# First loads, constants and late rows of an FFT and MoE kernel issued by GpSimd, zero rows stored later

## The chip, the cores and the metric

One core of a Trainium2 chip runs the kernel. The metric is the device time of one execution in microseconds: the median of the runs. A profiled execution gives, beside its time, the span from its first to its last instruction, the busy time of every engine, each DMA transfer and the clock granted to TensorE.

## The reference

An FFT along the sequence, a filter in the frequency domain, the inverse FFT, and then a mixture of experts in which each token goes to one expert, by the order of the sorted logits and a capacity of N / E tokens for each expert.

```python
X = np.fft.rfft(x, axis=1)                  # x: 8 x 2496 x 256, fp32
Y = X * (filt_r + 1j * filt_i)[None, :, :]
y = np.fft.irfft(Y, n=x.shape[1], axis=1)
x = y.reshape(B * S, D)                     # 19968 tokens x 256
logits = x @ w_gate                         # 8 experts
for idx in np.argsort(-logits.flatten()):   # greedy, cap = N // E
    tok, e = idx // E, idx % E
    ...
for e in range(E):
    h = np.maximum(x[mask[e]] @ w1[e], 0)   # 256 -> 1024
    out[mask[e]] = h @ w2[e]                # 1024 -> 256
```

## The kernel before

The sequence of 2496 is 39 x 64. The forward FFT is a step of 39 points (`s1`, a matmul with the constant `cS1`) and a step of 64 points (`s2`, with the per-column constants `cW`), then the product with the filter `F` (VectorE makes `P` and `Q`, GpSimd combines them at L246 and L247). `tr` transposes the result, adds the gate's columns (`pv`), and splits it into a high and a low part (`yh`, `yl`, at L278 and L279); `inv1` is the inverse step of 64 points with the constants `cE`, also in a high and a low part (`cEh`, `cEl`). Its result goes through the buffer `zt` (four of them) to DRAM (`zd`), and comes back as rows `z` for the inverse step of 39 points (`inv2_parts`, L399), whose result `xo` is stored as tokens `xs`. Each of the eight batch rows is a block `b`: its x comes in two halves `xr` (L208, each load cut into 112 partitions and 5), `s1` takes it in 11 tiles, `s2` in 5 groups of two halves, `tr` and `inv1` in 10 steps.

`run` (L406) gives each piece a slot and a priority and writes them out in that order; then the framework's scheduler sets the order on each engine by its own model of time. A queue's instructions start in order. Loads and stores from SP and ScalarE go round eight completion lanes (`DMAHW0` to `7` in the orders below), those from GpSimd round eight others (`DMASW0` to `7`); a transfer waits until the one before it on its lane has landed.

Before, SP issues all of x, the filter, the zero rows of `zd` (`zeros`, L195), the stores of `zt` and the loads of `z`. GpSimd issues the constants `cEh` and `cEl` in three parts (`load_E`, L189), and ahead of each stands a copy of one element of a product `P` into the target, so that the load waits for that product: the gate of that load.

Late in the FFT the last six blocks' rows `z` are kept back (`rest`, 30 of them): `more_z` (L354) and `more_z2` load eight of them into the places of `F`, `cW`, `Vh` and `Vl` when these are no longer read, and the other loads follow as `z` buffers come free. They are worked off beside the routing phase of the first expert. Then come the experts' matmuls (L854, L897) up to the end.

Of the kernel before, what the change touches and what calls it, by code (L numbers as in the profile page):

```python
# [12 lines left out]
B, N, D, E8, FF = 8, 2496, 256, 8, 1024  # L13

N1, N2, K1, J = 39, 64, 20, 64
# [114 lines left out]
class Fft:  # L130


    def __init__(s, tc, i, xs, zd, lg, pp):
        s.tc, s.nc, s.i, s.xs, s.zd, s.lg, s.pp = tc, tc.nc, i, xs, zd, lg, pp
        s.zw = s.zo = s.y7 = s.y9 = None
        s.xos = []
        s.nload = s.nstore = 0
        s.st_x = tc.nc.sync
        s.cps = tc.nc.vector.tensor_copy, tc.nc.scalar.copy
        s.y1c = {}  # L140
        s.Y1, s.yt, s.yd, s.z, s.xr, s.vs = {}, {}, {}, {}, {}, {}
# [29 lines left out]
    def consts2(s):  # L171
        nc, i = s.nc, s.i
        t = lambda n, sh, dt=F32: s.cp.tile(sh, dt, name=n)
        s.Vh, s.Vl = (s.cp.tile([128, K1, 64], F32R, name=n, tag=n, bufs=1) for n in ("Vh", "Vl"))
        s.id, s.gate = t("fid", [128, 128]), t("gate", [128, 2, 32])
        s.zero = s.zp.tile([120, 5, D], F32, name="xo", tag="xo", bufs=2)[:40, 0]
        s.cE = [t(n, [128, K1, 128], F32R) for n in ("cEh", "cEl")]
        for k, g in zip("FxFxFxFxFx", (0, 0, 1, 1, 2, 2, 3, 3, 4, 4)):
            if k == "F":
                nc.sync.dma_start(s.F[:, g], i['filt'][g].rearrange("p (h k j) -> p h k j", h=2, k=4))  # L180
            else:
                s.load_x(1, g // 3, *((g, 3) if g < 3 else (g - 3, 2)))
        make_identity(nc, s.id)
        nc.gpsimd.memset(s.gate, 0.0)
        nc.gpsimd.memset(s.zero, 0.0)
        for h in range(2):
            nc.scalar.dma_start(s.gate[:, h, :8], i['moe_w_gate'][128*h:128*h+128])

    def load_E(s, g, k0, k1):  # L189

        for c, nme in zip(s.cE, ("cEh", "cEl")):
            s.nc.gpsimd.tensor_copy(c[:1, k0, :1], s.yt[0, g, 0][:1, 0, :1])
            s.nc.gpsimd.dma_start(c[:, k0:k1], s.i[nme].rearrange("p (k q) -> p k q", k=K1)[:, k0:k1])

    def zeros(s):  # L195
        for zd in s.zd:
            s.nc.sync.dma_start(zd[:, N2:], s.zero.unsqueeze(1).to_broadcast([40, 2, D]))

    def load_x(s, b, h, k=0, parts=1):

        w = 24 - 5*h
        if k == 0:
            s.xr[b, h] = s.xp.tile([117, w, 2, N2], F32, name=f"xr{h}", bufs=2)
        xr = s.xr[b, h]
        v = s.i['x'][b].rearrange("p (q c n) -> p q c n", c=2, n=N2)
        q0, q1 = 4*((w+3)//4*k//parts), min(4*((w+3)//4*(k+1)//parts), w)
        for r in (slice(0, 112), slice(112, 117)):
            s.nc.sync.dma_start(xr[r, q0:q1], v[r, 24*h+q0:24*h+q1])  # L208

    def s1(s, b, t):  # L210

# [140 lines left out]
            nc.vector.tensor_copy(s.lg[:, b0:b1, g0:g1], p[:117].rearrange("p g (b e) -> p b g e", e=8))  # L352

    def more_z(s, units):  # L354

        f = s.wp.tile([128, 4, 5, D], F32, name="F", tag="F", bufs=1)
        w = s.wp.tile([128, 2, 5, D], F32, name="cW", tag="cW", bufs=1)
        y = s.wp.tile([128, 4, 5, D], F32, name="Y1", tag="Y1", bufs=2)
        s.xos = [y[:120, k] for k in range(4)]
        zs = [f[:120, k] for k in range(4)] + [w[:120, k] for k in range(2)]  # L360
        for u, z in zip(units, zs):
            s.load_z(*u, z)
# [5 lines left out]
    def load_z(s, b, t, z=None):  # L368
        g0, g1 = 5*t, min(5*t+5, G)
        if z is None:  # L370
            z = s.new_z((b, t) in s.rest)
        s.z[b, t] = z
        s.nc.sync.dma_start(z[:, :g1-g0], s.zd[b].rearrange("a (i g) c -> (a i) g c", i=3)[:, g0:g1])

    def new_z(s, late):
        zp, n = (s.zp, 3) if not late or s.nload % (3 + NZ) < 3 else (s.zw, NZ)
# [29 lines left out]
    def run(s, cp, wp, xp, ps, freed, prep, rest):  # L406
        s.cp, s.wp, s.xp, s.ps, s.rest = cp, wp, xp, ps, rest
        ev = []
        at = lambda slot, pr, fn, *a: ev.append((slot, pr, len(ev), fn, a))
        at(-12, 0, s.consts)  # L410
        for k in range(5):
            at(-12, 0, s.load_x, 0, k // 3, *((k, 3) if k < 3 else (k - 3, 2)))
        at(-12, 2, s.consts2)
        for g in range(1, 5):
            at(2*g - 2.1, 2.5, s.second, g)
        at(2.5, 1.5, s.load_E, 1, 0, 4)
        at(4.5, 1.5, s.load_E, 2, 4, 12)
        at(6.5, 1.5, s.load_E, 3, 12, K1)
        at(12, 9, s.zeros)
        for b in range(B):  # L420
            o = 10*b
            for t in range(11):
                at(o - 10 + t*10/11, 2, s.s1, b, t)
            if b + 2 < B:
                for h in range(2):
                    at(o - 4.4 + 4.5*h, 8, s.load_x, b + 2, h)
            for g in range(5):
                for dh in range(2):
                    at(o + 2*g + dh, 1, s.s2, b, g, dh)
                at(o + 2*g + 4.5, 3.5, s.trv, b, g)  # L430
            for q in range(10):
                at(o + q + 3, 3, s.tr, b, q)
                if b < B - 1 or q < 2:
                    at(o + q + I1, 4, s.inv1, b, q)
            for t in range(5):
                if b < B - NPOST:
                    z = Z0 + ZS * (5*b + t)
                    at(z - 4, 6, s.load_z, b, t)
                    at(z, 5, s.inv2, b, t)
        at(10*B - 9.5, 0, freed)  # L440
        for g in range(5):
            at(10*B - V1 + g*V1D, 3.8, s.v1, g, 0, B - 1)
            at(10*B - 5.2 + 2*g, 3.6, s.v1, g, B - 1, B)
        at(10*B - V2, 3.8, s.v2, 0, B - 1)
        at(10*B - V3, 3.8, s.v3, 0, B - 1)
        at(10*B - VP, 3.8, prep, 0, G * (B - 1))
        def act():
            s.cps = (s.nc.scalar.copy,) * 2
        at(10*B - AC, 0, act)
        for u in rest[:3]:  # L450
            at(10*B - 15, 9, s.load_z, *u)
        at(10*B - 0.8, 9, s.more_z, rest[3+NZ:9+NZ])
        at(10*B + 2.9, 3.61, s.more_z2, rest[9+NZ:3+NZ+MZ])
        at(10*B + 2.9, 3.6, s.v2, B - 1, B)
        at(10*B + 2.9, 3.62, s.v3, B - 1, B)
        at(10*B + 2.9, 3.64, prep, S - G, S)
        for q in (2, 3, 4):
            at(10*B + 2.9, 3.7 + 0.01 * q, s.inv1, B - 1, q)
        for e in sorted(ev, key=lambda e: e[:3]):
            e[3](*e[4])  # L460
# [665 lines left out]
```

## Time and profile before

| | |
|---|---|
| median of 3 runs | 1446.38 us (1446.09 to 1447.12) |
| profiled execution | 1445.38 us |
| its span | 1443.6 us |
| TensorE busy | 1386.9 us, 96% of the span |
| VectorE, ScalarE, GpSimd busy | 900.5, 680.5, 486.1 us |
| mean granted clock | 0.981 |

The FFT of the eight blocks takes the first 340 us, the late rows and the routing of the first expert go to about 434 us, and the rest are the experts. TensorE is busy nearly throughout, so time can only be won or lost where it waits, or where its clock is at the lower level. DMA busy share over 1 in a window means that transfers of the 16 engines overlap.

### The profile page before, as it was taken

To read this page: it belongs to the slowest core of one execution; us is meant where nothing else is said; L and a number is where in the kernel's file an instruction comes from. 1 tells how busy PE (TensorE), PEld (TensorE's weight loads), DVE (VectorE), ACT (ScalarE), POOL (GpSimd) and SP (SyncE) were. 2 spreads that over 40 slices of the span, in tenths; PEclk is the share of its full clock that TensorE was granted. 3 is DMA by queue.
4 is the path that set the end of the run, shared out by engine and by line. 5 is a ranking of instruction groups with operands and counts; after the bars stand their busy time and mean duration, and the time that the engine had idled before them with its cause. 6 is when DMAs were issued, how large, how long until landed. Compare 5 with 4: busy or idle time off the path is not lost. (4 is left out here: it accounts for less than half of the span.)

```text
span 1443.6 us, 27297 instructions
## 1 busy us (share of the span) xinstructions
PE 1386.9 (96%) x10338; PEld 1215.5 (84%) x10338; DVE 900.5 (62%) x2568; ACT 680.5 (47%) x1658; POOL 486.1 (34%) x538
## 2 busy tenths in 40 slices
PE   8799999998887999999999999999999999999998
PEld 7799988986446889888898988889898899899988
DVE  6476777776556778767856877776867735323231
ACT  6567666744464236325524533533633635433232
POOL 2343333442004315413531641433414333323212
PEclk9899999998997999999999999999999999999999
DMA  9977775558893103102112112111201321111100
GB/s 246 242 204 196 206 193 145 144 128 196 319 327 108 47 19 114 57 21 96 61 40 77 56 54 79 52 51 40 100 29 54 127 74 46 43 44 54 36 23 28
DMA packets 57992, 150.66 MB, mean 104 GB/s; under 512 B 10999, under 2 KB 32247, under 8 KB 54409
## 3 DMA queue, kind: packets, MB, share of 16 engines
q1 hardware_dynamic: 29068, 66.86, 17.5%
q0 software_dynamic: 18416, 60.37, 12.7%
q10 hardware_dynamic: 10377, 21.68, 4.6%
q8 instruction: 82, 1.34, 0.4%
q14 instruction: 49, 0.40, 0.1%
HBM read 85.23 MB, written 63.70 MB: 103 GB/s over the span
## 5 line engine op out<-in xcount | busy, mean ns | idle before, releaser
L897 PE MATMUL py<-w1h,hl 128*128 128x256 f32 x2496 | 485.8, 287 | 1.0 <-DVE hl L865 0.7
L897 PEld LDWEIGHTS py<-w1h,hl 128*128 128x128 f32 x2496 | 403.0, 191 | 7.3 <-issue 3.2
L897 PE MATMUL py<-w1l,hl 128*128 128x256 f32 (+1 forms) x1280 | 359.5, 283 | 0.0
L908 POOL DMA_INDIRECT out<-y,oid x160 | 168.8, 1055 | 507.0 <-ACT y L907 458.7
L860 ACT ACTIVATE hl<-pz 128x512 fp32r<-128x512 f32 (+1 forms) x320 | 187.4, 587 | 226.9 <-PE pz L854 203.6
L854 PE MATMUL pz<-xo,w0h 128*128 128x512 f32 (+1 forms) x640 | 263.9, 412 | 3.3 <-DVE hl L862 1.8
L862 DVE SCALAR_TENSOR_TENSOR hl<-pz,hl 128x512 fp32r<-128x512 f32 x256 | 175.4, 689 | 144.5 <-ACT hl L860 143.2
L854 PE MATMUL pz<-z,w0h 128*128 128x512 f32 (+1 forms) x640 | 248.7, 389 | 0.2 <-DVE z L836 0.2
L854 PE MATMUL pz<-xo,w0l 128*128 128x512 f32 (+1 forms) x640 | 248.5, 388 | 0.0
L897 PEld LDWEIGHTS py<-w1l,hl 128*128 128x128 f32 (+1 forms) x1280 | 241.7, 189 | 1.9
L818 POOL DMA_INDIRECT xg<-xs,xid x160 | 168.7, 1055 | 131.5 <-issue 51.5
L907 ACT COPY y<-py 128x256 f32<-128x256 f32 x152 | 56.6, 372 | 305.9 <-PE py L897 265.4
L854 PEld LDWEIGHTS pz<-xo,w0l 128*128 128x128 f32 x640 | 120.8, 189 | 24.0
L854 PEld LDWEIGHTS pz<-xo,w0h 128*128 128x128 f32 x640 | 121.7, 190 | 21.6 <-DVE hl L862 2.2
L854 PEld LDWEIGHTS pz<-z,w0h 128*128 128x128 f32 x640 | 121.6, 190 | 16.0 <-DVE z L836 0.9
L226 ACT COPY Y<-p 64x240 f32<-64x240 f32 (+1 forms) x302 | 115.3, 382 | 25.2 <-PE p L220 17.8
L246 POOL TENSOR_TENSOR P<-P 128x256 f32<-128x256 f32 x80 | 58.8, 735 | 184.9 <-DVE P L244 184.8
L557 DVE TENSOR_TENSOR Gm<-M,thr 117x1232 bf16<-117x1232 f32 (+2 forms) x80 | 105.5, 1329 | 0.2
L220 PE MATMUL p<-cS,xr 117*128 117x120 f32 x688 | 96.4, 279 | 9.2 <-DMA xr<-x 7.6
L220 PEld LDWEIGHTS p<-cS,xr 117*128 117x128 f32 x688 | 87.3, 195 | 13.7 <-issue 8.4
L238 PE MATMUL p<-cW,Y 128*128 128x128 f32 x640 | 89.9, 277 | 0.5 <-DVE Q L245 0.5
L238 PEld LDWEIGHTS p<-cW,Y 128*128 128x128 f32 x640 | 80.9, 192 | 6.0 <-issue 4.1
(220 smaller groups left out, 2013.7 us busy)
## 6 DMA issues: line engine op xcount, KB each, us to landing
z<-zd SPq DMA_DIRECT2D x26, 600.0 KB
zd<-zt SPq DMA_DIRECT2D x120, 128.0 KB
xs<-xo ACTq DMA_DIRECT2D x18, 600.0 KB
xr<-x SPq DMA_DIRECT2D x6, 1344.0 KB
xr<-x SPq DMA_DIRECT2D x6, 1064.0 KB
zd<-zt ACTq DMA_DIRECT2D x40, 128.0 KB
xs<-xo SPq DMA_DIRECT2D x8, 600.0 KB
xs<-Y ACTq DMA_DIRECT2D x6, 600.0 KB
```

The source lines that it names most:

```text
L220: s.lastmm = nc.tensor.matmul(p[:, q-q0, :120], xv[:, q-24*h], s.cS1, start=True, stop=True).ins
L226: c = (nc.vector.tensor_copy if (t == 5 if b else cp) else nc.scalar.copy)(dst, src)
L238: nc.tensor.matmul(p[:, k], s.Y1[b][:, 4*g+k, dh*128:dh*128+128], s.cW[:, 4*g+k], start=True, stop=True)
L246: nc.gpsimd.tensor_tensor(P[:, :, :64], P[:, :, :64], P[:, :, 64:], op=OP.subtract)
L557: nc.vector.tensor_tensor(Gm[:, s0:s1, :m], s.M[:, s0:s1].unsqueeze(2).to_broadcast([117, s1 - s0, m]), thr[:117].unsqueeze(1).to_broadcas ...
L818: s.lastg = s.nc.gpsimd.indirect_dma_start(out=xg[:n], out_offset=None, in_=s.xs, in_offset=bass.IndirectOffsetOnAxis(ap=ids[0][:n, t:t+1] ...
L854: nc.tensor.matmul(p[:, :n], w[:, sl], x[:, k, :n], start=m == 0, stop=m == 5)
L860: s.lasta = nc.scalar.activation(h[:, :n], p[:, :n], AF.Relu).ins
L862: s.R.low = nc.vector.scalar_tensor_tensor(l[:, :n], p[:, :n], 0.0, h[:, :n].bitcast(F32), op0=OP.max, op1=OP.subtract).ins
L897: nc.tensor.matmul(p[:a.stop-a.start], hs[g][f][:, a], b[:, 256*f:256*f+256], start=m == 0, stop=m == 8 * len(terms) - 1, skip_group_check ...
L907: s.lasta = nc.scalar.copy(y, p).ins
L908: st = nc.gpsimd.indirect_dma_start(out=out_rows, out_offset=bass.IndirectOffsetOnAxis(ap=ids[1][:w, 4*g+t:4*g+t+1], axis=0), in_=y[:w], i ...
```

## The change

The loads of the 112-partition parts of x of blocks 0 and 1, the filter and the inverse constants are issued by GpSimd. The constants' gates are gone, and their three parts stand between the filter groups and x of block 1. The identity is made after the second load in `consts2`'s list for block 1 instead of after all. The zero rows are held until `s.y1a`, the last copy of `s1` that ScalarE has when they are written. From `more_z` on, GpSimd issues the loads of `z` too.

```diff
-        s.st_x = tc.nc.sync
+        s.st_x, s.late = tc.nc.sync, False
...
-        for k, g in zip("FxFxFxFxFx", (0, 0, 1, 1, 2, 2, 3, 3, 4, 4)):
+        for k, g in zip("FxFxxFExFExFE", (0, 0, 1, 1, 2, 2, 0, 3, 3, 1, 4, 4, 2)):
             if k == "F":
-                nc.sync.dma_start(s.F[:, g], i['filt'][g].rearrange("p (h k j) -> p h k j", h=2, k=4))
+                nc.gpsimd.dma_start(s.F[:, g], i['filt'][g].rearrange("p (h k j) -> p h k j", h=2, k=4))
+            elif k == "E":
+                s.load_E(*((0, 4), (4, 12), (12, K1))[g])
             else:
                 s.load_x(1, g // 3, *((g, 3) if g < 3 else (g - 3, 2)))
-        make_identity(nc, s.id)
+            if (k, g) == ("x", 1):
+                make_identity(nc, s.id)
...
-    def load_E(s, g, k0, k1):
+    def load_E(s, k0, k1):
         for c, nme in zip(s.cE, ("cEh", "cEl")):
-            s.nc.gpsimd.tensor_copy(c[:1, k0, :1], s.yt[0, g, 0][:1, 0, :1])
             s.nc.gpsimd.dma_start(c[:, k0:k1], s.i[nme].rearrange("p (k q) -> p k q", k=K1)[:, k0:k1])
     def zeros(s):
-        for zd in s.zd:
-            s.nc.sync.dma_start(zd[:, N2:], s.zero.unsqueeze(1).to_broadcast([40, 2, D]))
+        with s.tc.issue_after(s.y1a):
+            for zd in s.zd:
+                s.nc.sync.dma_start(zd[:, N2:], s.zero.unsqueeze(1).to_broadcast([40, 2, D]))
...
-            s.nc.sync.dma_start(xr[r, q0:q1], v[r, 24*h+q0:24*h+q1])
+            (s.nc.gpsimd if b < 2 and r.start == 0 else s.nc.sync).dma_start(xr[r, q0:q1], v[r, 24*h+q0:24*h+q1])
...
     def more_z(s, units):
+        s.late = True
...
-        s.nc.sync.dma_start(z[:, :g1-g0], s.zd[b].rearrange("a (i g) c -> (a i) g c", i=3)[:, g0:g1])
+        (s.nc.gpsimd if s.late else s.nc.sync).dma_start(z[:, :g1-g0], s.zd[b].rearrange("a (i g) c -> (a i) g c", i=3)[:, g0:g1])
...
-        at(2.5, 1.5, s.load_E, 1, 0, 4)
-        at(4.5, 1.5, s.load_E, 2, 4, 12)
-        at(6.5, 1.5, s.load_E, 3, 12, K1)
```

The scheduler then orders the instructions anew. GpSimd at the start, before: the gates (L192) and loads (L193) of the first constants stand between the products of the first filter groups.

```order
L246 TENSOR_TENSOR P<-P 128x4x64 [waits DVE_49]
L192 CAST cEh<-P 1x1 [waits Pool_49]
L192 CAST cEl<-P 1x1
L247 TENSOR_TENSOR P<-Q 128x4x64 [waits DVE_49]
L193 DMA cEh<-cEh 128x512 [waits Pool_49]
L193 DMA cEl<-cEl 128x512 [waits Pool_49]
```

The same place after, the end of the loads: `xr_152` is the second half of block 1, `cEh` and `cEl` of 128x512 are the first part of the constants.

```order
L195 DMA cEh<-cEh 128x512 [waits DMASW3_49]
L195 DMA cEl<-cEl 128x512 [waits DMASW4_49]
L211 DMA xr_152<-x 112x1024 [waits DMASW5_49]
L180 DMA F<-filt 128x1024 [waits DMASW6_49]
L195 DMA cEh<-cEh 128x1024 [waits DMASW7_49]
L195 DMA cEl<-cEl 128x1024 [waits DMASW0_49]
L211 DMA xr_152<-x 112x1408 [waits DMASW1_49]
L180 DMA F<-filt 128x1024 [waits DMASW2_49]
L195 DMA cEh<-cEh 128x1024 [waits DMASW3_49]
L195 DMA cEl<-cEl 128x1024 [waits DMASW4_49]
L187 MEMSET gate 128x64
```

The first products (L249) come behind these rows, after the memsets and the identity; 21 loads stand ahead of them, of which the first eight (block 0's five, filter group 0, block 1's first piece, filter group 1) wait for no lane.

SP at the start, before: block 1's last piece (`xr_147`), then block 2's halves (`xr_225`, `xr_292`), then the zero rows.

```order
L180 DMA F<-filt 128x1024 [waits DMAHW3_49]
L208 DMA xr_147<-x 112x1408 [waits DMAHW4_49]
L208 DMA xr_147<-x 5x1408 [waits DMAHW5_49]
L208 DMA xr_225<-x 112x3072 [waits DMAHW6_49,PE_49]
L208 DMA xr_225<-x 5x3072 [waits DMAHW7_49]
L208 DMA xr_292<-x 112x2432 [waits DMAHW0_49,PE_49]
L208 DMA xr_292<-x 5x2432 [waits DMAHW1_49]
L197 DMA zd_60<-xo 40x2x256 [waits DMAHW2_49,Pool_49]
```

After, block 2 is `xr_231` and `xr_298`, block 3's first half `xr_479`.

```order
L211 DMA xr_152<-x 5x1408 [waits DMAHW4_49]
L211 DMA xr_231<-x 112x3072 [waits DMASW2_49,DMASW1_49,DMAHW5_49,DMASW0_49,PE_49]
L211 DMA xr_231<-x 5x3072 [waits DMAHW6_49]
L211 DMA xr_298<-x 112x2432 [waits DMASW4_49,DMAHW7_49,DMASW3_49,PE_49]
L211 DMA xr_298<-x 5x2432 [waits DMAHW0_49]
L200 DMA zd_60<-xo 40x2x256 [waits DMAHW2_49,Pool_49]
L200 DMA zd_61<-xo 40x2x256 [waits DMAHW4_49]
L211 DMA xr_479<-x 112x3072 [waits DMASW6_49,DMAHW1_49,DMASW1_49,DMAHW5_49,DMASW0_49,PE_49]
```

Block 2's x no longer stands behind block 1's x and the filter, and two of the eight zero rows stand ahead of block 3.

TensorE at the same time, before: the first tile of block 2 (`p_697`) is followed by inverse steps (L293) and gate columns (L266).

```order
L220 MATMUL p_697<-cS_87,xr_225 128x120 [waits DMAHW6_49,DMAHW7_49,PE_49,Activation_49]
L220 MATMUL p_697<-cS_87,xr_225 128x120 x3
L293 MATMUL pa<-yh,cEh 128x256 [waits DMASW0_49]
L293 MATMUL pa<-yl,cEh 128x256
L257 MATMUL pa<-fid,P 128x128 x4
L266 MATMUL pv<-P,gate 32x128 x8
```

After: tiles 8 to 10 of block 1 (`p_576`, `p_627`, `p_671`) and 0 and 1 of block 2 (`p_691`, `p_738`) stand in a row, and the first gate columns (L269) behind them; inverse steps (L296) come later still.

```order
L223 MATMUL p_576<-cS_87,xr_152 128x120 [waits DMAHW4_49,DMASW1_49,Activation_49]
L223 MATMUL p_576<-cS_87,xr_152 128x120 x3
L223 MATMUL p_627<-cS_87,xr_152 128x120 [waits Activation_49]
L223 MATMUL p_627<-cS_87,xr_152 128x120 x3
L223 MATMUL p_671<-cS_87,xr_152 128x120 [waits PE_49,Activation_49]
L223 MATMUL p_671<-cS_87,xr_152 128x120 x2
L223 MATMUL p_691<-cS_87,xr_231 128x120 [waits DMAHW5_49,DMAHW6_49,PE_49,Activation_49]
L223 MATMUL p_691<-cS_87,xr_231 128x120 x3
L223 MATMUL p_738<-cS_87,xr_231 128x120 [waits PE_49,Activation_49]
L223 MATMUL p_738<-cS_87,xr_231 128x120 x3
L269 MATMUL pv<-P,gate 32x128 [waits DMAHW1_49]
```

Up to that point ten second steps have been issued before (one of them in progress) and seven after, four transposes before and two after, two gate groups and two inverse steps before and none after.

GpSimd's late rows, before: the last two products of block 7, then the splits of its last inverse steps (L279) and nothing between them.

```order
L246 TENSOR_TENSOR P<-P 128x4x64 [waits DVE_49]
L247 TENSOR_TENSOR P<-Q 128x4x64 [waits DVE_49,Pool_49]
L279 TENSOR_TENSOR yl<-Y_3932,yh 128x512 [waits PE_49,Activation_49] x4
L279 TENSOR_TENSOR yl<-P,yh 128x512 [waits PE_49,Activation_49]
L998 COPY sidx<-xo 1x1 [waits Activation_49,Pool_49]
```

After: four loads into `F`'s place stand between these two products, and the loads of `z` among the splits.

```order
L249 TENSOR_TENSOR P<-P 128x4x64 [waits DVE_49]
L376 DMA F<-zd_63 120x1280 [waits DMASW2_49,DMASW0_49,DVE_49]
L376 DMA F<-zd_63 120x1280
L376 DMA F<-zd_63 120x512
L376 DMA F<-zd_64 120x1280 [waits DMASW3_49]
L250 TENSOR_TENSOR P<-Q 128x4x64 [waits Pool_49]
L376 DMA Vh<-zd_64 120x1280 [waits DMASW4_49,DVE_49,PE_49]
L376 DMA Vl<-zd_64 120x512 [waits DMASW5_49,PE_49]
L282 TENSOR_TENSOR yl<-Y_3926,yh 128x512 [waits PE_49,Activation_49] x3
```

## Rows read from the trace of the kernel before

**Rows 1.** The page, part 1, first entry: busy us (share of the span) xinstructions.

```profile
PE 1386.9 (96%) x10338; PEld 1215.5 (84%) x10338; DVE 900.5 (62%) x2568; ACT 680.5 (47%) x1658; POOL 486.1 (34%) x538
```

**Rows 2.** TensorE's waits, 0 to 100 us: us in total, times, longest us.

```profile
PE p L220 <- DMA xr<-x: 7.6, 5, 3.7
PE pa L293 <- DVE zt L305: 3.9, 1, 3.9
```

**Rows 3.** TensorE's waits, 80 to 300 us, the first row.

```profile
PE pa L293 <- DVE tab L525: 1.3, 1, 1.3
```

**Rows 4.** TensorE's timeline: start, us, line, operation, [idle before <- what ended it].

```profile
13.84 2.02 PE L220 MATMUL p<-cS,xr 117*128 117x120 f32 x16 [0.19 <-PE p L220]
...
46.68 2.03 PE L220 MATMUL p<-cS,xr 117*128 117x120 f32 x8 [3.69 <-DMA xr<-x]
...
71.05 0.58 PE L293 MATMUL pa<-yh,cEh 128*128 128x256 f32 x1 [3.91 <-DVE zt L305]
```

**Rows 5.** Stretches: us, busy us by engine, PEclk, DMA share, GB/s.

```profile
2.00:45.00 43.00, 34.96 (x283) 31.97 (x282) 28.69 (x64) 33.05 (x89) 14.84 (x26) 1.00 1.06 254
69.00:76.00 7.00, 4.95 (x24) 4.95 (x25) 5.64 (x11) 1.36 (x3) 2.91 (x4) 0.51 0.62 157
358.00:392.00 34.00, 32.24 (x153) 16.88 (x150) 19.47 (x65) 16.78 (x36) 0.00 (x0) 1.00 0.96 338
```

**Rows 6.** Timeline of GpSimd and ScalarE.

```profile
22.72 0.72 POOL L246 TENSOR_TENSOR P<-P 128x256 f32<-128x256 f32 x1 [21.07 <-DVE P L244]
...
29.34 0.74 POOL L193 DMA_DIRECT2D cEh<-cEh  x1
30.07 0.59 POOL L193 DMA_DIRECT2D cEl<-cEl  x1
...
38.65 6.19 ACT L226 COPY Y<-p 64x240 f32<-64x240 f32 x16
...
327.98 1.00 POOL L247 TENSOR_TENSOR P<-Q 128x256 f32<-128x256 f32 x1
```

**Rows 7.** SP's timeline: block 2's first half, and the late loads into `F`.

```profile
27.92 0.69 SPq L208 DMA_DIRECT2D xr<-x  x2
...
327.72 1.94 SPq L373 DMA_DIRECT2D F<-zd  x4
```

**Rows 8.** DMA queues, 36 to 44 us: packets, MB, share of 16 engines.

```profile
q1 hardware_dynamic: 168, 1.49, 89.5%
q0 software_dynamic: 180, 0.34, 20.7%
```

**Rows 9.** TensorE's timeline, 51 to 59 us and at 330 us.

```profile
51.95 0.28 PE L293 MATMUL pa<-yh,cEh 128*128 128x256 f32 x1
...
52.66 1.05 PE L238 MATMUL p<-cW,Y 128*128 128x128 f32 x8
53.55 0.60 PE L220 MATMUL p<-cS,xr 117*128 117x120 f32 x4
...
54.54 1.06 PE L238 MATMUL p<-cW,Y 128*128 128x128 f32 x8
55.44 0.60 PE L257 MATMUL pa<-fid,P 128*128 128x128 f32 x4
55.88 1.06 PE L238 MATMUL p<-cW,Y 128*128 128x128 f32 x8
...
57.54 0.65 PE L266 MATMUL pv<-P,gate 128*32 128x128 f32 x16
58.12 0.70 PE L220 MATMUL p<-cS,xr 117*128 117x120 f32 x4
...
330.18 1.04 PE L257 MATMUL pa<-fid,P 128*128 128x128 f32 x8
```

**Rows 10.** ScalarE's timeline at 395 us.

```profile
395.29 1.84 ACT L400 COPY xo<-pv 120x512 f32<-120x512 f32 x4 [7.15 <-DMA xs<-Y]
```

**Rows 11.** SP's waits, 300 to 480 us, the first row.

```profile
SPq L373 <- PE pv L399: 35.4, 12, 8.9
```

## The prediction

> **What bounds the kernel now.** I read the page's first part, then TensorE's waits, then the timeline where those waits lie. TensorE is busy for 96% of the span [rows 1], so only a stretch in which it waits can give time back. In the first 100 us two waits matter: 7.6 us in all for pieces of x, the longest 3.7 us, and once 3.9 us for a vector copy of `zt` [rows 2]. From 80 to 300 us its longest wait is 1.3 us [rows 3]: the FFT stage is then bound by TensorE, and whatever is won or lost before 80 us is carried unchanged to the end of that stage.
>
> The waits stand at two places [rows 4]: at 46.68 us the first step of block 2 starts 3.69 us late, when its x has landed, and at 71.05 us an inverse step starts 3.91 us late. The second is a blocked store: the copy needs a `zt` buffer whose store stands on SP behind zero rows and x loads. After it the clock is at 0.51 of full speed, the 1.2 GHz level, from 69 to 76 us [rows 5]; from 71.05 on, 4.9 us of work then take twice as long as at 2.4 GHz, 2.5 us lost. From 2 to 45 us the DMA engines are full (share 1.06) and move 254 GB/s [rows 5], so the start is bound by bytes: what counts is the order in which they come.
>
> **The change part by part.** Sizes come from the shapes in the orders, times 4 bytes: an x block is 2.58 MB (four pieces of 0.48, one of 0.66), block 2's halves 1.44 and 1.14, a filter group 0.52, the inverse constants 0.52, 1.05 and 1.05, the small constants 0.27.
>
> *Issue time.* GpSimd takes 0.74 us for such a load [rows 6], SP some 0.35 (0.69 us for two [rows 7]). 21 loads come to GpSimd at the start; they are hidden, since nothing there needs GpSimd before 22.72 us [rows 6], and a load takes longer to move than to issue (0.48 MB at 254 GB/s is 1.9 us). Taking the gates away saves six tiny copies off the path. Both: nothing.
>
> *Order of the bytes.* Before, block 2's x came behind block 1 and the filter on SP's queue, issued at 27.92 us [rows 7]. Now SP has only five-row pieces ahead of it, and issues it when block 0's tiles have read the buffer: the first half when tile 5 is done, at 13.84 us [rows 4], the second at about 19. From then on two queues compete. How they share is in the trace: from 36 to 44 us SP's queue moved 168 packets and GpSimd's 180 [rows 8], turn by turn, but 1.49 MB against 0.34, since SP's rows were 9.7 and 12 KB and GpSimd's 2 KB. Block 1's rows are 4 KB: block 2 gets three bytes of four and overtakes block 1.
>
> So I count bytes. GpSimd issues its last constant only when the 13th load has landed (the lane wait on `DMASW4` in its order, shown with the change). Ahead of that landing are block 0, three filter groups, three pieces of block 1 and the first constants (2.58 + 1.57 + 1.44 + 0.52), the small ones and all of block 2: 8.96 MB, at 254 GB/s from 2 us on 37.3 us. GpSimd's first product then starts at about 39 us, not at 22.72 [rows 6], and the transposes of block 0 come at about 43.
>
> The last piece of block 1 is the 18th load: 0.48 + 0.52 + 1.05 + 0.66 MB more, and ahead of it goes the first half of block 3 (1.44), which SP issues at about 39 us behind two zero rows, again with 12 KB rows, and some 0.2 of zero rows: 13.3 MB, 54 us. TensorE's new order puts block 1's tile 8 (`p_576`) ahead of all gate and inverse products, and it waits for that piece. Then tiles 8, 9, 10 of block 1 and 0, 1 of block 2 follow, paced by ScalarE's four copies for each (16 in 6.19 us [rows 6], 1.55 a tile) and two PSUM buffers: tile 1 of block 2 ends at about 60 us. Before, it ended at 54.54 [rows 9], with more done: two second steps (0.89 each), two transposes (0.44), two gate groups (0.58) and two inverse steps (0.71), 5.2 us by the differences of starts in [rows 9]. The start falls back by 5.5 + 5.2 = 10.7 us.
>
> What comes back: the 3.69 us wait lies inside that count. The 3.91 us and the 2.5 at the low clock I take as gone: the stores of `zt` now come when block 3 and the zero rows are issued, and no inverse step starts before 60. That is 6.4, and the start costs 10.7 - 6.4 = **+4.3**. Bounds: if the new queue were not outrun, the last piece would be there at (13.3 - 2.58 - 1.44 - 0.2) / 0.254 + 2 = 38 us and the start would gain at most 3.69 + 3.91 + 2.5 and as much again for the clock after the first wait, about -12.6; if `zt` still blocked, +10.7. I stay with the count, whose share is a row of this trace.
>
> *Zero rows later.* 0.66 MB, 2.6 us of transfers; they are stored among block 3 and before the first inverse stores, so they stay in the same stretch: nothing beyond the count.
>
> *Late rows.* The loads of the late blocks wait for TensorE to free a buffer, on SP as on GpSimd. The end of this stage is set by bytes: DMA share 0.96 from 358 to 392 us [rows 5], and ScalarE then waits 7.15 us for stores [rows 10]. Another queue moves no byte faster; a separate set of lanes frees the loads from waiting for stores, but the row that shows such a stall (395.29 us) waits for the stores themselves. What it costs: four loads into `F` now stand before the last product of block 7 on GpSimd (its late rows, shown with the change). Before, that product ran at 327.98 us for 1.00 us [rows 6] and SP issued those loads at 327.72 [rows 7]. Now 4 x 0.59 to 0.74 us come first [rows 6], 2.4 to 3.0 us; it ends at 331.4 to 332.0, and the transposes that began at 330.18 [rows 9] wait 1.2 to 1.8. They lead to the gate values and the routing, and nothing there hides it: **+1.5**, from 0 (the stage ends by bytes and absorbs it) to +4 (also the two last `yl` splits wait behind a load).
>
> Sum: 1445.38 (profiled execution: span 1443.6 and 1.8 around it) + 4.3 + 1.5 = 1451.2; the median of the runs is 1.0 above that execution, so **1452.2 us**.
>
> **The rivals.** *Not outrun (faster).* SP's load of block 2 comes no sooner, or GpSimd's rows get more than a turn each, so block 1 is there by about 38 us, and TensorE's two waits end: 1446.4 - 12.6 + 1.5 = 1435; with half of it 1441. For it: GpSimd has up to eight loads under way from the start, with no gate. Against it: 168 packets to 180. It decides at the landing of block 1's last piece: by the count each microsecond earlier gives one back, so the change gains below about 48 us.
>
> *Lost and given back (no change).* Both orders move the same bytes over the same engines, and by 65 us both have everything; if TensorE catches up, since nothing makes it wait after 60, only the late 1.5 is left: 1446 to 1449. The Trainium skill, page DMA: Bandwidth & Descriptors, section Issuing engines are not separate DMA queues, says that starting transfers from several engines saves only the time to issue them. By that rule alone the order of the bytes would not count, and this case would be it. The trace agrees on the sum of bytes; that an issuer changes whose bytes come first is what the 168 and 180 packets show.
>
> *Late loads block (slower still).* GpSimd runs in order: a late load that waits for a buffer holds back the `yl` splits of the last block, and their inverse steps hold TensorE. SP's waits of this kind are 35.4 us in 12, the longest 8.9 [rows 11]; two of the mean length more give 1458.
>
> **How the numbers follow.** Forecast 0.45, not outrun 0.28, given back 0.17, late loads block 0.10. I predict 1452.2. The forecast's own range, from the landing time (50 to 57 us) and the late bounds, is 1446 to 1458. For 8 in 10 I cut half of the first rival and the top of the last: 1438 to 1461. Within 0.2% (2.9 us, about what this measurement can tell from no change) lie the third case and a tenth of the forecast: 0.22. Faster 0.28, slower 0.50.
>
> **What would show it.** GpSimd's first product after 35 us; block 2's first half landing before block 1's second piece; TensorE waiting for `xr` at tiles 0, 2, 6 and 8 of block 1, last near 54 us; no wait for `zt` near 70; GpSimd's last product of block 7 some 2.5 us behind VectorE's. If TensorE waits little for `xr` before 40 us, the share was wrong and with it the sign.

## Result and profile after

The kernel after takes 1459.7 us (median of 9 runs, 1455.31 to 1465.57) against 1446.38 before: ratio 1.0099, 95% interval 1.0082 to 1.0115, some 13 us slower. The forecast was 5.8 us slower, 1452.2, with a range up to 1461. The direction held and the size did not: 13.3 us stand against 5.8, and the median lies 1.3 us under the top of the range. Two terms of the sum were too small and one cost was not in it; the experiments and the traces say which.

The profiled execution took 1458.04 us, its span is 1456.2. TensorE is busy as before, 96% (compare [rows 1]):

```profile
PE 1390.6 (96%) x10338; PEld 1219.7 (84%) x10338; DVE 900.9 (62%) x2568; ACT 680.8 (47%) x1658; POOL 504.9 (35%) x570
```

So the loss is again made of waits. TensorE's longest waits from 0 to 100 us (us in total, times, longest us; compare [rows 2]):

```profile
PE p L223 <- DMA xr<-x: 11.7, 3, 9.6
PE p L223 <- ACT Y L229: 2.4, 4, 0.8
PE p L241 <- DVE Q L248: 2.2, 2, 1.3
PE pa L260 <- POOL P L250: 1.3, 1, 1.3
```

Three waits for x with 11.7 us together, one of them 9.6, stand where before had five with 7.6, and the 3.9 us for `zt` are gone. The timeline of TensorE shows where (start, us, line, operation, [idle before <- what ended it]):

```profile
25.13 1.06 PE L241 MATMUL p<-cW,Y 128*128 128x128 f32 x8
35.83 2.04 PE L223 MATMUL p<-cS,xr 117*128 117x120 f32 x8 [9.64 <-DMA xr<-x]
...
47.44 0.44 PE L260 MATMUL pa<-fid,P 128*128 128x128 f32 x2 [1.32 <-POOL P L250]
...
54.06 1.13 PE L241 MATMUL p<-cW,Y 128*128 128x128 f32 x8 [0.92 <-DVE Q L248]
56.45 1.13 PE L241 MATMUL p<-cW,Y 128*128 128x128 f32 x8 [1.26 <-DVE Q L248]
57.42 1.95 PE L223 MATMUL p<-cS,xr 117*128 117x120 f32 x16
60.13 0.93 PE L223 MATMUL p<-cS,xr 117*128 117x120 f32 x6 [0.77 <-ACT Y L229]
61.72 1.15 PE L223 MATMUL p<-cS,xr 117*128 117x120 f32 x8 [0.66 <-ACT Y L229]
63.10 1.15 PE L223 MATMUL p<-cS,xr 117*128 117x120 f32 x8 [0.23 <-ACT Y L229]
...
297.85 0.83 PE L223 MATMUL p<-cS,xr 117*128 117x120 f32 x6
```

At 25 us TensorE runs dry and waits for block 1's second piece until 35.83. Tile 8 of block 1 comes at 57.42 and tile 1 of block 2 ends at 64.25, against 54.54 before [rows 9]. The last row is the last tile of the first step of all eight blocks. In the kernel before the same row is this:

```profile
288.20 0.83 PE L220 MATMUL p<-cS,xr 117*128 117x120 f32 x6
```

At both times TensorE has issued the same number of matmuls of every kind, so the start has cost 297.85 - 288.20 = 9.65 us. This row serves below as the mark of the start. It is sharper than the ratios: kernels with the same loads at the start reach it within 0.4 us of one another, while a ratio of five rounds is uncertain by 0.15 to 0.25%, 2 to 3.5 us.

The engine that holds the list of loads, GpSimd (compare [rows 6]):

```profile
29.66 0.53 POOL L195 DMA_DIRECT2D cEh<-cEh  x1 [6.68 <-DMA F<-filt]
35.87 0.53 POOL L195 DMA_DIRECT2D cEl<-cEl  x1 [5.69 <-DMA xr<-x]
...
43.33 0.53 POOL L195 DMA_DIRECT2D cEl<-cEl  x1 [0.43 <-DMA cEl<-cEl]
...
44.62 2.09 POOL L249 TENSOR_TENSOR P<-P 128x256 f32<-128x256 f32 x3
```

It waits in turn for the lanes of its earlier loads, issues its last constant at 43.33 and begins its first product at 44.62 instead of 22.72. From 22 to 34 us, while both queues have work, they share so (packets, MB, share of 16 engines; compare [rows 8]):

```profile
q1 hardware_dynamic: 219, 2.18, 72.5%
q0 software_dynamic: 224, 0.81, 26.3%
```

SP's queue (q1) moves block 2 and GpSimd's (q0) moves block 1, the filter and the constants. They take turns packet for packet, and as block 2's packets are the larger ones, 73% of the bytes go to it. In numbers of the stretch from 25 to 45 us (us, busy us by engine PE, PEld, DVE, ACT, POOL, PEclk, DMA share, GB/s), after and then before:

```profile
25.00:45.00 20.00, 8.58 (x52) 8.08 (x50) 4.11 (x11) 8.04 (x22) 4.26 (x10) 0.74 1.10 252
```

```profile
25.00:45.00 20.00, 16.39 (x143) 14.65 (x141) 14.74 (x31) 17.89 (x49) 12.89 (x24) 1.00 1.09 244
```

The DMA engines do as much in both; the other engines do about half or less, and after the long wait TensorE's clock falls to the lower of its two levels for part of the stretch.

At the other end, the first gather's transposes and the last matmul of the experts, after and before:

```profile
449.53 1.51 PE L832 MATMUL ptr<-id,xg 128*128 128x128 f32 x6 [11.10 <-DMA xg<-xs,xid]
...
1448.44 0.28 PE L897 MATMUL py<-w1l,hl 128*64 128x256 f32 x1
```

```profile
439.02 1.51 PE L832 MATMUL ptr<-id,xg 128*128 128x128 f32 x6 [10.66 <-DMA xg<-xs,xid]
...
1437.85 0.28 PE L897 MATMUL py<-w1l,hl 128*64 128x256 f32 x1
```

From the first of these rows to the second it is 998.9 us after and 998.8 before: the experts are untouched. The 12.6 us between the two spans are 9.65 at the start, 0.9 from there to the gathers, 0.1 in the experts, and 2.0 behind the last matmul (7.8 against 5.8 us to the end of the span). The 0.9 says little: in the seven kernels below that have all late rows on GpSimd, the kernel after among them, this stretch takes 149.7 to 153.2 us in single executions. The 2.0 have a plain source. The last scatter lands 3.7 us behind the last matmul in both, and what ends last is GpSimd's closing DRAIN. After and before (calls, then shortest, median and longest in ns; the longest is the closing one):

```profile
L1122 POOLq DRAIN  x3: 46/97/5710, 1449.7 to 1455.9; - x3
```

```profile
L1122 POOLq DRAIN  x3: 97/194/3311, 1439.1 to 1443.2; - x3
```

It grows with the number of plain loads that GpSimd has issued in the whole program, whichever they are: 7 loads and 3.3 us in the kernel before, 17 and 3.7 in c_x0F_only, 22 and 3.9 in a_late_sp, 30 and 4.6 in b_late_pool, 45 and 5.7 in the kernel after. No kernel was built to test this alone.

One reading of the code ahead of the prediction has to be put right. The zero rows are not held by `s.y1a`. That is an instruction of ScalarE, and in SP's order after, shown ahead, the first zero row waits for its lane and for GpSimd and not for ScalarE. What makes the rows late is that they wait for the zeros, which GpSimd writes behind its list. SP's longest wait from 0 to 70 us (total, times, longest):

```profile
SPq L200 <- POOL xo L188: 22.1, 1, 22.1
```

### The profile page after: what moved, and what is told of

It reads as the page before. It is cut to its first block, busy times and chain, and to the rows that moved or that the text cites. A ratio compares the mean times of both kernels' runs of the same rounds, so it can differ in the third digit from the quotient of the medians.

```text
span 1456.2 us, 27303 instructions
## 1 busy us (share of the span) xinstructions
PE 1390.6 (96%) x10338; PEld 1219.7 (84%) x10338; DVE 900.9 (62%) x2568; ACT 680.8 (47%) x1658; POOL 504.9 (35%) x570
## 5 line engine op out<-in xcount | busy, mean ns | idle before, releaser
L223 PE MATMUL p<-cS,xr 117*128 117x120 f32 x688 | 98.9, 288 | 16.1 <-DMA xr<-x 11.7
L249 POOL TENSOR_TENSOR P<-P 128x256 f32<-128x256 f32 x80 | 58.5, 732 | 150.3 <-DVE P L247 150.3
L223 PEld LDWEIGHTS p<-cS,xr 117*128 117x128 f32 x688 | 90.4, 203 | 21.0 <-issue 12.9
```

The source lines that it names most:

```text
L223: s.lastmm = nc.tensor.matmul(p[:, q-q0, :120], xv[:, q-24*h], s.cS1, start=True, stop=True).ins
L249: nc.gpsimd.tensor_tensor(P[:, :, :64], P[:, :, :64], P[:, :, 64:], op=OP.subtract)
```

## Experiments

The start is taken as the row of the last first-step tile (288.20 before), the end as the ratio to the kernel before on the same chip.

| kernel | last first-step tile, us | ratio | 95% interval |
|---|---|---|---|
| after | 297.85 | 1.0099 | 1.0082 to 1.0115 |
| a_x1_sp | 294.52 | 1.0069 | 1.0046 to 1.0092 |
| a_x2_pool | 296.94 | 1.0093 | 1.0070 to 1.0117 |
| a_E_gated | 291.53 | 1.0058 | 1.0036 to 1.0081 |
| a_late_sp | 298.20 | 1.0059 | 1.0037 to 1.0081 |
| a_E_last | 296.85 | 1.0061 | 1.0038 to 1.0083 |
| a_prod_dve | 294.09 | 1.0043 | 1.0026 to 1.0060 |
| c_xF_only | 291.63 | 0.9987 | 0.9968 to 1.0005 |
| c_x0F_only | 288.09 | 1.0015 | 0.9993 to 1.0037 |
| b_late_pool | 288.27 | 1.0028 | 1.0015 to 1.0040 |
| b_latez | 287.95 | 0.9994 | 0.9979 to 1.0009 |
| b_zeros_late | 287.63 | 1.0003 | 0.9986 to 1.0019 |
| b_zeros_E | 287.93 | 0.9972 | 0.9956 to 0.9989 |

Names with a_ or c_ start from the kernel after, those with b_ from the kernel before. c_xF_only, c_x0F_only and b_zeros_E ran on a chip on which the kernel before takes 1463 us; their ratios are taken on that chip, and no trace of the kernel before was kept from it. The mark can be compared all the same: a_E_gated and c_xF_only, with the same loads at the start, reach it 0.1 us apart on two chips.

**a_x1_sp**: block 1's x on SP's queue again.

```diff
-            (s.nc.gpsimd if b < 2 and r.start == 0 else s.nc.sync).dma_start(xr[r, q0:q1], v[r, 24*h+q0:24*h+q1])
+            (s.nc.gpsimd if b < 1 and r.start == 0 else s.nc.sync).dma_start(xr[r, q0:q1], v[r, 24*h+q0:24*h+q1])
```

> The kernel after, with x of block 1 on SP's queue again (block 0, the filter and the constants stay on GpSimd), so that block 2's x stands behind block 1's in one queue. Theory A (block 2's 12 KB rows on another queue overtake block 1; that is the 9.6 us wait at 26 to 36 us): the wait goes, block 1 lands by 30 us, and the time falls by 6 to 9 us against the kernel after, to about 1451. Theory B (GpSimd, held in its list of loads until 43 us by its lanes, is late with its first products, and that sets the start): the list keeps 15 loads, its first product comes well after 30 us, and the time stays within 3 us of the kernel after, 1456 to 1460.

Measured: 294.52 at the mark, 3.3 us of the 9.65 won.

```profile
294.52 0.83 PE L223 MATMUL p<-cS,xr 117*128 117x120 f32 x6
```

TensorE's longest wait for x up to 100 us is now 2.8 us, so the overtaking is undone. But GpSimd's first product comes at 39.20, and TensorE waits 9.3 us for it. Theory A names a third of the loss, not the whole; theory B is not ruled out by it. The edit also takes five loads out of GpSimd's list (16 stay, not 15), so the 3.3 us are those of moving block 1, not of the overtaking by itself.

**a_x2_pool**: block 2's x too at the end of GpSimd's list (`b < 3` in the same line).

> The kernel after, with x of block 2 too at the end of GpSimd's list of loads. Theory A: block 1 is not overtaken, its pieces land in the order of issue, the 9.6 us wait at 26 us goes; block 2 comes some 10 us later instead, which the tiles of block 1 cover in part: 1450 to 1455. Theory B: GpSimd's products stand behind two more loads, its first product comes at 44 us or later, and the time is 1458 to 1463.

Measured: 296.94 and 1.0093, next to nothing. Block 1 is no longer overtaken (2.2 us of waits for x in three), but block 2, issued at 34.76, lands at 60.9, and TensorE then waits 7.4 us:

```profile
60.97 3.31 PE L223 MATMUL p<-cS,xr 117*128 117x120 f32 x14 [7.41 <-issue]
```

The profile names no releaser for that row; the landing, read from the transfer's own records, is 0.1 us before it. Order alone, with all the bytes still ahead, only moves the wait. Theory A in its simple form falls.

**a_E_gated**: the constants behind their gates again, everything else as after.

```diff
-        for k, g in zip("FxFxxFExFExFE", (0, 0, 1, 1, 2, 2, 0, 3, 3, 1, 4, 4, 2)):
+        for k, g in zip("FxFxxFxFxF", (0, 0, 1, 1, 2, 2, 3, 3, 4, 4)):
...
+            s.nc.gpsimd.tensor_copy(c[:1, k0, :1], s.yt[0, g, 0][:1, 0, :1])
...
+        at(2.5, 1.5, s.load_E, 1, 0, 4)
+        at(4.5, 1.5, s.load_E, 2, 4, 12)
+        at(6.5, 1.5, s.load_E, 3, 12, K1)
```

> The kernel after, with the six loads of the inverse constants behind GpSimd's first products again, with their gates. Theory A: block 2 overtakes block 1 as before, the wait near 26 to 36 us stays at 7 to 10 us; GpSimd's products come 10 to 20 us earlier, which is worth at most the 3.6 us lost between 42 and 66 us: 1455 to 1459. Theory B: with GpSimd free the start loses only what before loses: 1447 to 1451.

```profile
291.53 0.83 PE L222 MATMUL p<-cS,xr 117*128 117x120 f32 x6
```

6.3 us of the 9.65 come back, with a 7.4 us wait up to 38.28 still there (by the transfer's own records block 1's second piece lands at 38.0; the profile names the load of `gate`). GpSimd's first product comes at 28.92. So the early constants, through GpSimd or through their bytes, are the larger part. The gates that I had priced at nothing kept them out of the way.

**a_late_sp**: the late rows on SP (`s.late = True` left out).

> The kernel after, with the late rows z on SP again. If the four loads ahead of GpSimd's last product cost what was forecast, 1.5 us come back (1456.5 to 1458.5 against 1459.7 of the kernel after, ratio 0.998 to 0.9995). If the late rows cost nothing because bytes and stores set that stage, the ratio is 1.000. If GpSimd's late loads hold back more than that, 3 us or more come back.

Measured: 298.20 at the mark, as expected unchanged; ratio 1.0059 against 1.0099. 0.4% come back, 5.8 us between the ratios with some 4 of uncertainty, more than the 1.5 forecast. In its trace the gathers come at 445.88 instead of 449.53 and the span ends 5.9 us behind the last matmul instead of 7.8.

**b_late_pool**: the kernel before with the late rows on GpSimd.

```diff
     def more_z(s, units):
+        s.late = True
...
-        s.nc.sync.dma_start(z[:, :g1-g0], s.zd[b].rearrange("a (i g) c -> (a i) g c", i=3)[:, g0:g1])
+        (s.nc.gpsimd if s.late else s.nc.sync).dma_start(z[:, :g1-g0], s.zd[b].rearrange("a (i g) c -> (a i) g c", i=3)[:, g0:g1])
```

> The kernel before, with the late rows z alone issued by GpSimd. The kernel after with these rows on SP again won 0.4% back, more than was forecast. If that is a cost of the late rows by themselves (GpSimd holds loads that wait for a buffer ahead of its last products and splits), this kernel loses 3 to 5 us: ratio 1.002 to 1.0035. If it was only how the late stage took up a later start, the ratio is 1.000 to 1.001.

Measured: 1.0028, 4.0 us, and 1 lies outside the interval. The late rows cost by themselves; 1.3 us of it are the longer closing DRAIN. Its profiled execution (1445.92 us) is the fastest of its 12 runs (median 1449.60) and reaches the gathers at 438.88, no later than before, so its trace can show where a delay arises but not that it is carried on. The place where it arises is TensorE's order at the end of the transform. After:

```profile
345.15 1.12 PE L565 MATMUL rt<-A,Gm 117*48 117x128 bf16 x9 [2.81 <-DVE A L541]
...
349.08 2.95 PE L344 MATMUL pv<-fid,Y 8*120 8x8 f32 x22 [0.67 <-ACT Y L330]
...
352.98 0.64 PE L296 MATMUL pa<-yh,cEh 128*128 128x256 f32 x1
```

The same in a_late_sp:

```profile
345.17 2.95 PE L344 MATMUL pv<-fid,Y 8*120 8x8 f32 x22 [0.67 <-ACT Y L330]
348.05 0.93 PE L564 MATMUL rt<-A,Gm 117*48 117x128 bf16 x9
...
349.43 0.64 PE L296 MATMUL pa<-yh,cEh 128*128 128x256 f32 x1
```

With the late loads on SP the nine routing matmuls (`rt`) come behind the last gate columns and wait for nothing. With them on GpSimd the scheduler puts the routing matmuls ahead, presumably because it expects block 7's last product later; there they wait 2.81 us for VectorE's `A`, and the last gate columns and inverse steps queue behind: 352.98 against 349.43, 3.6 us, though the start of a_late_sp is 0.35 later. b_late_pool has the same rows with the same wait of 2.82, and its inverse steps begin at 343.41 against 339.65 before.

**b_latez**: as b_late_pool, but `s.late = True` at the end of `more_z`, so that the loads into `F` and `cW` stay on SP.

> The kernel before, with the late rows z on GpSimd from the loads into the places of Vh and Vl on; the six loads into the places of F and cW, which stand ahead of GpSimd's last products, stay on SP. TensorE's order at the end of the transform is then that of before: the nine routing matmuls stand behind the last gate columns again, not ahead of them. If the 0.28% of the kernel with all late rows on GpSimd comes from that order (the routing matmuls wait 2.8 us for VectorE's A and push the last inverse steps back by 3.8 us), the ratio is 1.000, within 0.001. If it comes from GpSimd holding back loads and splits behind one another, it stays at 1.002 to 1.003.

Measured: 0.9994 (0.9979 to 1.0009). The order is that of before again:

```profile
336.55 2.95 PE L341 MATMUL pv<-fid,Y 8*120 8x8 f32 x22 [0.67 <-ACT Y L327]
339.43 1.16 PE L565 MATMUL rt<-A,Gm 117*48 117x128 bf16 x9
...
341.03 0.64 PE L293 MATMUL pa<-yh,cEh 128*128 128x256 f32 x1
```

The other 17 late loads on GpSimd cost nothing that this ratio can tell, with all of its waiting for buffers. The six ahead of its last products bring the 0.3%, and with them the changed order comes and goes. That they cost by way of this order is likely and not shown: whether they would cost the same with TensorE's order held fixed was not tried.

**a_E_last**: the list as `FxFxxFxFxFEEE`, the constants without gates behind filter and block 1.

> The kernel after, with the six loads of the inverse constants at the end of GpSimd's list, behind the filter and block 1, still without gates. Theory D (2.6 MB of constants, which nothing needs before the first inverse step, come ahead of x): block 1 lands some 5 to 10 us earlier, and about as much is won as with the gates, 4 to 6 us: 1453 to 1456. Theory B (GpSimd is held by its list until its last constants are issued): 21 loads stay in the list, the last waits for the landing of the 13th, GpSimd's first product comes at 36 to 44 us as now, and the time stays at 1457 to 1461.

Measured: at the mark 296.85, 1.0 us won; the ratio, 1.0061, would allow 5. The two hardly agree: a win of 1.0 us would leave 1.0092, and the ratio's interval ends at 1.0083; its profiled execution, 1456.21, lies 1.9 above its median. GpSimd is held longer still:

```profile
48.78 2.09 POOL L249 TENSOR_TENSOR P<-P 128x256 f32<-128x256 f32 x3
```

By the start, theory B has it; the rest of the ratio stays open. Beside a_E_gated it says more. Up to the constants the two lists are the same, TensorE's waits for x add up to 14 to 15 us in both, and block 1's second piece lands at 39.6 here and at 38.0 there. But GpSimd's first product comes 19.9 us later than there, and the mark 5.3 us later.

**a_prod_dve**: the list as after, but identity and zeros made ahead of the list, and the products of block 0's first two filter groups on VectorE.

```diff
+        make_identity(nc, s.id)
+        nc.gpsimd.memset(s.gate, 0.0)
+        nc.gpsimd.memset(s.zero, 0.0)
         for k, g in zip("FxFxxFExFExFE", (0, 0, 1, 1, 2, 2, 0, 3, 3, 1, 4, 4, 2)):
...
+        e = nc.vector if b == 0 and g < 2 else nc.gpsimd
+        e.tensor_tensor(P[:, :, :64], P[:, :, :64], P[:, :, 64:], op=OP.subtract)
+        e.tensor_tensor(P[:, :, 64:], Q[:, :, :64], Q[:, :, 64:], op=OP.add)
```

> The kernel after, with the products of the first two filter groups of block 0 on VectorE instead of GpSimd, and the identity and the zeros made ahead of the list: GpSimd is held as before, but the first transposes no longer wait for it. The bytes and their order stay. Theory B (held GpSimd): the first transposes come at about 30 us instead of 47, and 3 to 6 us are won: 1454 to 1457. Theory D (bytes of the constants and of block 2 ahead of block 1): TensorE still waits for x near 26 to 36 us and the time stays within 2 us: 1458 to 1461.

Measured: 294.09 at the mark, 3.8 us won; ratio 1.0043. Its TensorE timeline:

```profile
29.53 0.38 PE L260 MATMUL pa<-fid,P 128*128 128x128 f32 x2
...
41.72 2.03 PE L222 MATMUL p<-cS,xr 117*128 117x120 f32 x8 [5.58 <-DMA xr<-x]
...
56.33 0.55 PE L296 MATMUL pa<-yh,cEh 128*128 128x256 f32 x1 [5.19 <-DMA cEh<-cEh]
59.58 0.58 PE L296 MATMUL pa<-yh,cEl 128*128 128x256 f32 x1 [2.48 <-DMA cEl<-cEl]
```

The transposes come at 29.53 instead of 47.44 although not a byte less is moved. But the order of the bytes changed, though it was expected to stay. The zeros are made early, so SP stores its zero rows at once, and block 2's x stands behind them:

```profile
10.40 11.49 SPq L199 DMA_DIRECT2D zd<-xo  x8
22.07 12.97 SPq L210 DMA_DIRECT2D xr<-x  x6
```

Block 2's first half is issued at 22.07 instead of 16.31, block 1's second piece is there by 26.8 instead of 35.6, and GpSimd's list ends at 34.4 instead of 43.9. So the 3.8 us belong to the freed products and to the changed order together, and this kernel does not separate them. What is left waits for x, and then for the constants themselves.

**c_xF_only**: a_E_gated and a_late_sp together; x of blocks 0 and 1 and the filter stay on GpSimd.

> The kernel after with both undone: the constants behind their gates, and the late rows on SP. Only x of blocks 0 and 1 and the filter stay on GpSimd. If the parts add up, what is left of the start (3.4 us at the last first-step tile in the kernel with the gates alone) is all that is left: ratio 1.001 to 1.0025. If the late stage takes up so small a delay, as it took up 3 us of the 10 with the late rows alone on SP, the ratio is 1.000. If the parts overlap, it stays at 1.004 or more.

Measured: 291.63 at the mark, as a_E_gated; ratio 0.9987 (0.9968 to 1.0005). By the ratio nothing is left at the end of a start that is 3.4 us late. Where it would be taken up is not shown: this kernel and the next one, on the same chip, are 3.5 us apart at the mark and 5.4 at the gathers (438.04 and 432.66).

**c_x0F_only**: the same with `b < 1`, block 1's x on SP.

> As the kernel that leaves x of blocks 0 and 1 and the filter on GpSimd, but with x of block 1 on SP's queue, so that block 2 can't overtake it. If overtaking is what is left of the start, TensorE's wait for x near 30 us (7.4 us with the gates alone) goes and the ratio is 0.999 to 1.0005; if it is the slower first tiles, which the list on GpSimd brings in any case, the ratio stays that of the other kernel.

```profile
288.09 0.83 PE L222 MATMUL p<-cS,xr 117*128 117x120 f32 x6
```

At the mark 0.1 us ahead of before: nothing is left of the loss. Its ratio (0.9993 to 1.0037) tells no difference. With it the four kernels make a square at the mark:

| | x of block 1 on GpSimd | on SP |
|---|---|---|
| constants in the list, no gates | 297.85 | 294.52 |
| constants behind gates | 291.53 | 288.09 |

Down the columns 6.3 and 6.4 us, along the rows 3.3 and 3.4: at the mark the two changes add up, and together they are the whole loss of the start. This is a balance, not the start of before again. In c_x0F_only the wait for `zt` is gone, and another has come: ScalarE's copies stand behind its own loads of `gate`, which wait for loads of x, and TensorE waits for ScalarE (first ScalarE, then TensorE):

```profile
23.23 4.39 ACTq L188 DMA_DIRECT2D gate<-moe_w_gate  x2
27.66 1.54 ACT L228 COPY Y<-p 64x240 f32<-64x240 f32 x4 [10.29 <-DMA xr<-x]
...
28.47 4.46 PE L222 MATMUL p<-cS,xr 117*128 117x120 f32 x22 [6.73 <-ACT Y L228]
```

GpSimd's first product comes at 36.23 there, later than in a_E_gated, without harm to the mark. So a late first product is not a price by itself; what it costs depends on what TensorE can do meanwhile.

**b_zeros_late**: the kernel before with the zeros made behind a product of block 1, so that the zero rows really come later.

```diff
-        nc.gpsimd.memset(s.zero, 0.0)
...
+        s.nc.gpsimd.tensor_copy(s.zero[:1, :1], s.yt[1, 0, 0][:1, 0, :1])
+        s.nc.gpsimd.memset(s.zero, 0.0)
```

> The kernel before, with the zero rows truly stored later: the zeros themselves are made behind a product of block 1, so that SP issues block 3's x and the first inverse stores ahead of them. If the 3.9 us wait for zt at 71 us in the kernel before comes from stores behind the zero rows and x on SP, it goes, with the 2.4 us at the lower clock: 1439 to 1443, ratio 0.996 to 0.9985. If block 3's x alone holds the stores, the wait stays and the ratio is 1.000.

Measured: 1.0003. The wait for `zt` is gone, and waits for the constants took its place (TensorE, 0 to 100 us):

```profile
PE pa L294 <- DMA cEl<-cEl: 6.2, 2, 5.1
PE p L221 <- DMA xr<-x: 3.8, 4, 1.4
PE pa L294 <- DMA cEh<-cEh: 2.4, 1, 2.4
```

**b_zeros_E**: the same with each gate of the constants one product earlier (`load_E` at 1.5, 2.5, 4.5 with groups 0, 1, 2).

> The kernel before with the zeros made late, and the gates of the constants one product earlier each. The zeros alone ended the wait for zt, but waits for cEh and cEl (8.6 us) took its place. If these come from the constants' issue, earlier gates win what the zeros should have won: 1439 to 1443, ratio 0.995 to 0.998. If the bytes of block 2 ahead of them decide, the wait moves to x and the ratio stays at 1.000 or above.

Measured: 0.9972 (0.9956 to 0.9989), the one version that beats both kernels. Its mark at 287.93 is only 0.3 us ahead of before, and TensorE still waits for x (7.2 us in five) and for `cEl` (4.0), so where the 0.28% comes from is not shown.

## Why the prediction was right and wrong

*What bounds the kernel* held: only waits of TensorE counted, it waits for nothing from 80 to 300 us, so that nothing there gave back what the start had lost, and the experts took the same time.

*Order of the bytes* held as a fact: the queues took turns by packets, block 2 overtook block 1, the first step ran dry and block 1's last piece landed at 53.6 us (forecast 54). Moving block 1's x, which brings the overtaking, costs 3.3 to 3.4 us at the mark (a_x1_sp, and the lower row of the square), near the 4.3 that I put down for the whole start.

*The step that failed* is "Issue time": "Taking the gates away saves six tiny copies off the path. Both: nothing", and that the 21 loads are hidden because nothing needs GpSimd before 22.72 us. The same text then has GpSimd's first product at 39, 16 us late (it came at 44.62), and gives that no price beyond the 5.2 us of work not yet done. At the mark the constants in the list without gates cost 6.3 us (a_E_gated). Moving them behind x and the filter won 1.0 of it (a_E_last). The other 5.3 lie between a_E_last and a_E_gated, and there GpSimd's first product differs by 19.9 us, while block 1's last piece lands at 49.8 and 46.9. So the larger part is put down to the held GpSimd; a share of bytes, in that last piece, is in it too, and nothing here separates the two. The cover of the loads was the time before 22.72; the list ran to 43.9. Issuing from GpSimd had a second price that the same step left out: the closing DRAIN, 2.4 us longer, of which 2.0 reach the end of the span.

In the sum it shows at one term: tile 1 of block 2 ends at 64.25, not 60, though the piece it waited for had landed as forecast. In between stand two second steps, which wait for VectorE's `Q` (0.92 and 1.26 us in the rows above). VectorE is busy without a gap from 51.6 to 56.3: among other work it has the splits of the late transposes ahead of the second `Q`.

```profile
54.44 1.27 DVE L282 TENSOR_TENSOR yl<-pa,yh 128x512 fp32r<-128x512 f32 x2
55.63 0.67 DVE L248 TENSOR_TENSOR Q<-p,F 128x512 f32<-128x512 f32 x1
```

The start falls back by 64.25 - 54.54 + 5.2 = 14.9 instead of 10.7. What came back was 14.9 - 9.65 = 5.3, not 6.4: the wait for `zt` did go, and no part of 65 to 80 us ran at the lower clock, as forecast, but parts of 25 to 65 us did.

*Late rows*: +1.5 was forecast with 4 as its upper end; the cost is 4.0 (b_late_pool; 2.2 to 5.8 by its interval), 1.3 of it in the closing DRAIN. The mechanism was another. The transposes are hardly later, since TensorE's order moved with them (a pair of transposes at 339.83 and six matmuls at 341.11). What the traces show instead is that order: I read GpSimd's rows of the change there and not TensorE's, where nine routing matmuls change sides and the inverse steps come 3.6 us later.

*Zero rows*: priced at nothing. In the kernel before, storing them later changes nothing that the ratio can tell (b_zeros_late); in the kernel after it was not tried by itself. Their reason was misread.

*The rivals.* "Not outrun" fell with the 9.6 us wait. "Lost and given back" may be right in part and is not shown: by the ratio c_xF_only starts 3.4 us late and ends level, and in a_late_sp 10.0 us at the mark are 6.9 at the gathers, in one execution. The kernel after gave nothing back by its trace. The rule behind that rival (the Trainium skill, DMA: Bandwidth & Descriptors, section Issuing engines are not separate DMA queues, by which several issuing engines save only the time to issue) does not give this case: with the same bytes, the choice of issuer moves the mark by 3.3 us in either row of the square. "Late loads block" named the splits; in b_latez the loads among the splits, waiting as they do, cost nothing that the ratio can tell.

Open: the ratios of a_E_last and a_prod_dve. Added to the late rows' 4.0 us, what they lose at the mark (8.65 and 5.9 us) would make 12.7 and 9.9; measured are 8.8 and 6.2, with intervals that end at 12.0 and 8.7.

## What to carry to other kernels

A load moved to a compute engine is paid for by the instructions behind it: find the time at which the list ends, by its completion lanes, not by its issue time, and price the first thing that then comes late. Here such loads were paid for once more at the end of the program, some 0.06 us each. A gate that looks like overhead may be what keeps bytes that nobody needs yet out of the way of those that somebody does. And where a planner orders the engines, look at the engine that bounds the kernel as well as at the one that was changed: here 17 late loads cost nothing that could be measured, and six, which came with a swap of nine matmuls on another engine, cost 0.3%.

## What was not expected of the hardware

Half a megabyte can be under way for a long time on a queue that shares the engines with larger rows: GpSimd's load of the second filter group, issued at 5.22 us, held its lane until 29.4, and block 1's second piece, issued at 7.39, until 35.6, while the DMA engines moved 244 to 247 GB/s throughout. It is the packet that is shared: with 12 and 9.7 KB packets against 4 KB ones the two queues had 219 and 224 packets and 2.18 and 0.81 MB, from 22 to 34 us. In c_x0F_only, where both move rows of 4 KB and few larger ones, they had 465 and 464 packets and 1.86 and 1.83 MB from 14 to 28 us (SP's queue first).

GpSimd's closing DRAIN took 3.3 us after 7 plain loads in the program and 5.7 after 45, with values in between for the counts in between; in the kernel after, that is the end of the span.

A held queue also holds others: SP stood 22.1 us before a zero row that waited for one memset of 0.3 us on GpSimd.

The chip on which c_xF_only, c_x0F_only and b_zeros_E ran differs from the others in the experts and not at the start: a_E_gated and c_xF_only, the same at the start, reach the mark at 291.53 and 291.63, while from the first gather's transposes to the last matmul these three take 1014 to 1018 us, against 998 to 1001 in all other kernels. Why was not looked into; it is the reason for ratios.
